# Two-branch spectral mixing on one core: 64x64 matmul tiles, a split inverse radix, contiguous transposes and a new hand-written order

## The chip, the core and the metric

The kernel runs on one core of a Trainium2 chip. A core has TensorE (PE; its weight loads are shown apart as PEld), VectorE (DVE), ScalarE (ACT) and GpSimd (POOL), and SyncE (SP), whose queue issues most DMAs. The metric is the device time of one execution in microseconds (us), the median over several runs. All data is fp32; a matmul of fp32 shows in the trace as two records (two passes).

## The reference

```python
x = A_x                                    # 1 x 2048 x 512, row index = time, column = channel
g = sigmoid((x * gate_w).sum(-1, keepdims=True))
# a: 2-D real FFT over time and channel, times a complex weight, and back
X = rfft2(x) * (A_w_r + 1j * A_w_i)
a = irfft2(X, s=(2048, 512))
# b: state-space convolution along time, and a skip
K = 2 * einsum("dn,dnl->dl", C, exp(A * dt * pos)).real
b = irfft(rfft(u, 4096) * rfft(K, 4096), 4096)[:, :2048] + u * D_skip     # u = x
out = g * a + (1 - g) * b
```

Where a channel's `dt` is so small that `K` is constant over the 2048 steps, the convolution is a running sum over time, scaled by one number a channel. The kernel counts the channels for which that holds; when it holds for all 512, as with these inputs, it uses running sums, and a general path in an `If` at the end is skipped.

## The kernel before, in words

Four pieces of work share the engines.

*Input transform.* The input comes in parts (`PARTS`), is folded (`fold`: sum and difference of two halves of the channels, on VectorE `f` or GpSimd `F`), goes through a first radix step over 32 time values (`C_`, TensorE), and is transposed in 32x32 blocks from PSUM into `AR` (`c_a`, VectorE).

*Frequency units.* Nine units (`UNITS`; index 0 is a half unit of 64 rows, the others have 128). Each goes: `P_` second time step on TensorE, `t_a` copy to SBUF on ScalarE, `D_` channel transform on TensorE, `d_a` copy of one half on ScalarE, `Z_` sums and differences on VectorE, `W_` twice (letters `W`, `U`), the products with the weights, on VectorE, `p_a` and `g_a` sums and differences on GpSimd, `h_a` a fix of row 0 on ScalarE, `I_` inverse channel transform on TensorE, `i_a` copy on ScalarE, `V_` sum and difference into `AI` on VectorE.

*Running sum.* For four groups of 128 channels: `load_x`, scaling on ScalarE into PSUM (`x_a`), a running sum on VectorE (`scan`), a skip scaling in place on ScalarE (`skip`), and an accumulating DMA on GpSimd's queue that adds the running sum onto the input (`both`), or VectorE instead (`skip2`). `G_` is the gate: 16 matmuls in column tiles of 32, a sigmoid, and a DMA that spreads it.

*Inverse along time and output.* `B_` second inverse time step (TensorE), a copy back (`e_a`, ScalarE), a transposition in 32x32 blocks in place (`b_a`, VectorE). `Y_` turns the running-sum branch (TensorE transposes), `s_a` scales it by 1 - g (ScalarE); `Q_` is the last time step (TensorE), and `q_a` (VectorE), or `a_a` with `A_a` (ScalarE, GpSimd), adds both and stores.

The order on every engine is the order of the words in `PLAN`: a letter for the function and a number for its argument. PSUM has four buffers of two banks, taken in turn by all of this (`psum`), so a step can wait for the reader of the buffer's last content. `blk` has 13 SBUF buffers, `w` four.

Of the kernel before, what the change touches and what calls it, by code (L numbers as in the profile page):

```python
# [15 lines left out]
P = 128  # L30
L = 2048
# [8 lines left out]
F1 f0 C0 c0 C1 R2 f2 R5 R3 f3 l2 c1 F4 C2 c2 f5 C4 N0 F6 X0 l3 R4 C5 R1 c4 C6 f8 C8 N1 N2 G4 F9 R0 c5 l0 X1 l1 c8 c6  # L40
C9 C3 c9 f7 N3 x0 X2 C7 c3 R6 c7 P1 P0 J0 G5 x1 t1 J1 t0 D1 m0 m1 J2 x2 m2 P2 P4 L2 L1 D0 R9 d1 z1 Z1 y1 t2 D2 t4 W1
U1 L3 d0 z0 p1 Z0 L0 y0 W0 l4 d2 z2 Z2 y2 U0 P6 P5 U2 R8 g1 P3 t5 t6 D5 W2 R7 L4 p0 g0 t3 X3 x3 l5 h1 D3 z3 m3 d3 d5
l7 L5 Z3 z5 y3 h0 W3 U3 l6 p2 I1 i1 V1 G0 P7 g2 Z5 o3 p3 o0 L6 y5 G1 G2 t7 W5 D4 d4 I0 g3 U5 p5 g5 h3 D6 z4 Z4 S3 D7
i0 V0 y4 U4 o1 L7 W4 d7 z6 G3 d6 Z6 h5 l8 y6 z7 r0 P8 p4 t8 B1 W6 Z7 e1 y7 h2 U6 g4 I5 i5 o2 p6 D8 z8 L8 W7 g6 U7 p7
d8 h4 V5 I3 r1 i3 V3 x4 o4 I2 i2 B3 e3 I4 Z8 y8 m4 g7 h6 i4 V2 x6 W8 h7 I6 i6 U8 V6 V4 I7 S2 p8 i7 V7 m6 k6 g8 h8 B2
B6 e6 e2 I8 i8 v8 B5 x7 S1 e5 B4 x5 m7 j8 e4 w8 E8 o5 K8 H8 S0 B7 e7 m5 r2 k7 Y4 Y7 Y1 Y6 b1 s7 s4 Y3 s3 Y0 s0 Y2 Y5
b6 s6 s1 b2 b3 b0 b4 s5 b5 b7 Q6 s2 Q0 q6 q0 Q5 q5 Q3 q3 Q7 Q4 q4 a7 Q2 A7 q2 Q1 q1
# [9 lines left out]
def _consts():  # L57
# [38 lines left out]
    s2e = s2[:17].reshape(17, 128, 128).transpose(1, 0, 2)  # L96
# [15 lines left out]
    s2p = s2p.transpose(1, 0, 2)  # L112
# [10 lines left out]
    s1a = np.zeros((32, 2, 2, 16, 2, 2, 32, 2))  # L123
    for g in range(2):
        s1b[:, g, :, :, :, g] = s1i[32 * g:32 * g + 32]
        for e in range(2):
            for dh in range(2):
                s1a[:, g, :, :, e, dh, :, g] = s1i[32 * g:32 * g + 32, :, :16] * 2 / 512 * (-1) ** (e * dh)
    s1b = s1b.reshape(32, 128, 64).transpose(1, 0, 2)
    s1a = s1a.reshape(32, 128, 128).transpose(1, 0, 2)  # L130
# [16 lines left out]
        "c_s1e": f32(s1e.reshape(128, 128)), "c_s1f": f32(s1f.transpose(1, 0, 2)), "c_s2e": f32(s2e), "c_s2": f32(s2),  # L147
        "c_s2p": f32(s2p), "c_s2q": f32(s2q), "c_s1b": f32(s1b), "c_s1a": f32(s1a), "c_dfw": f32(dfw), "c_dbw": f32(dbw),
# [5 lines left out]
def body(ctx: ExitStack, tc: tile.TileContext, x, xg, xt, w, wh, prms, vecs, gw, dskip,  # L154
         c_s1e, c_s1f, c_s2e, c_s2, c_s2p, c_s2q, c_s1b, c_s1a, c_dfw, c_dbw, c_pos, c_eye, out):
# [14 lines left out]
    AI = keep.tile([P, 17, D], F32, name="AI")  # L170
    VA = AI[:, 0:16].rearrange("p s (e d) -> p (s e) d", e=2)
# [31 lines left out]
    with tc.manual_schedule():  # L203
# [3 lines left out]
        for i, k in enumerate(PARTS):  # L207
            nc.sync.dma_start(X[:, 64 * k.start:64 * k.stop], x[:, 64 * k.start:64 * k.stop])
# [7 lines left out]
        V.memset(one, 1.0)  # L216
# [15 lines left out]
        def C_(q):  # L232
            n = 32 * (PARTS[q].stop - PARTS[q].start)
            p = t_["c", q] = psum("p_s1")
            for u in range(2):
                T.matmul(p[:, u, :n], s1e, t_["f", q][:, u, :n], start=True, stop=True)  # L236

        def c_a(q):
            n = PARTS[q].stop - PARTS[q].start
            V.transpose(AR.rearrange("p s (u d) -> p u d s", u=2)[:, :, PARTS[q]], t_["c", q][:, :, :32 * n].rearrange("p u (b d) -> p u d b", d=n))  # L240

# [33 lines left out]
        def x_a(r):  # L275
            t_["v1", r] = psum("p_x").rearrange("p u n -> p (u n)")
            S.activation(t_["v1", r], part(r), AF.Copy, scale=s0[:, coef(r):coef(r) + 1])  # L277

        def scan(r):
            if r % 2 == 0:  # L280
                t_["v", r // 2] = work.tile([P, 2, 1024], F32, tag="v", name="v", bufs=NV)
            v = t_["v0", r] = t_["v", r // 2][:, r % 2]
            V.tensor_tensor_scan(v, one.broadcast_to([P, 1024]), t_["v1", r], t_["v0", r - 1][:, 1023:1024] if r % 2 else 0.0, op0=ALU.mult, op1=ALU.add)  # L283
# [4 lines left out]
        def both(k):  # L288
            G.dma_start(XT[:, k], t_["v", k].rearrange("p h l -> p (h l)"), accum_op=ALU.add)
# [42 lines left out]
        def load_w(u):  # L332
# [5 lines left out]
            t_["w", u] = t.rearrange("p (o r a k) -> p o r a k", o=2, r=2, a=2)  # L338
# [6 lines left out]
        def P_(u):  # L345
            pr = UNITS[u]
            p = t_["pt", u] = psum("p_t").rearrange("p k (q c r) -> p (k q) c r", q=2, c=2)
            for v in range(nrow(pr) // 64):
                sl, k = (0, 16) if pr == 8 else (2 * pr + v, 2 * pr + v)
                for q in range(4):  # L350
                    T.matmul(p[:, q, :, 64 * v:64 * v + 64], AR[:, 16 * (q // 2) + sl, 128 * (q % 2):128 * (q % 2) + 128], s2e[:, k], start=True, stop=True)  # L351
# [18 lines left out]
        def d_a(u):  # L370
            ds = t_["ds", u] = short("ds")
            S.copy(ds[..., :nrow(UNITS[u])], parts(u)[:, :, 0:4:3])


        def Z_(u):
            n = nrow(UNITS[u])
            p, re = parts(u), t_["ds", u][..., :n]
            V.tensor_tensor(p[:, :, 0:4:3], p[:, :, 1:3], re, op=ALU.add)  # L378
# [416 lines left out]
```

## Time and profile before

| quantity | value |
|---|---|
| median of 3 runs | 148.23 us (147.55 to 148.67) |
| span of the profiled execution | 146.8 us, 1834 instructions |
| VectorE busy | 113.8 us in 134 instructions |
| TensorE busy | 112.6 us in 611 records |
| ScalarE busy | 70.5 us in 136 |
| GpSimd busy | 57.4 us in 57 |
| HBM | 17.93 MB read, 4.19 MB written |

The span runs from the first to the last instruction of the profiled execution, 1.4 us less than the median of the timed runs. Rows of the trace have a start, a length in us, an engine, a line of the kernel, an operation, the tiles it writes and reads, and how often; in square brackets stands the idle time before it and what ended it. Rows of groups have a line, a shape, a count, busy us and the mean ns of one, then the idle time before.

### The profile page before, as it was taken

The page shows a single profiled execution, that of the slowest core. Times are in us where ns is not written, and L with a number is a line of the kernel's source. Part 1 is how long each engine was busy: PE and PEld are TensorE (multiplying, and loading weights), DVE is VectorE, ACT ScalarE, POOL GpSimd, SP SyncE. Part 2 cuts the span into 40 slices and gives each one's busy share as a digit, 9 for nine tenths or more (in the row PEclk, how much of TensorE's full clock was granted, in tenths as well). Part 3 has the DMA queues.
Part 4 walks back from the last instruction along what each step waited for, and adds up shares of the span by engine and source line. Part 5 has one row for each costly group of instructions (what it writes and reads, how often), then busy time and mean ns, then how long its engine had stood idle before and what let it go on. Part 6 is the DMA issues. An engine that isn't in the chain of part 4 may idle for free.

```text
span 146.8 us, 1834 instructions
## 1 busy us (share of the span) xinstructions
PE 112.6 (77%) x611; PEld 86.1 (59%) x611; DVE 113.8 (78%) x134; ACT 70.5 (48%) x136; POOL 57.4 (39%) x57
## 2 busy tenths in 40 slices
PE   7936976399989998959888878997805975999600
PEld 7811352098978982858378577462405964888400
DVE  0369999995788597759798995979689997695900
ACT  0003000337375969496789765398610699504000
POOL 0306850100059993976999979200200000003300
PEclk9999999959999999999999999999975899999985
DMA  4999999992105870404793898000191000158690
GB/s 114 318 275 418 391 417 387 413 416 99 37 7 173 287 292 0 143 5 146 132 225 91 273 214 210 4 0 0 40 214 36 0 0 0 57 205 318 223 354 19
DMA packets 9427, 25.52 MB, mean 174 GB/s; under 512 B 1568, under 2 KB 2624, under 8 KB 8512
## 3 DMA queue, kind: packets, MB, share of 16 engines
q1 hardware_dynamic: 8976, 22.16, 42.2%
q0 software_dynamic: 432, 3.15, 10.9%
q8 instruction: 7, 0.11, 0.3%
q14 instruction: 12, 0.10, 0.2%
HBM read 17.93 MB, written 4.19 MB: 151 GB/s over the span
## 4 chain that ended last, share of the span: by engine, by line
DVE 31%; PE 30%; ACT 17%; DMA 9%; issue 5%; POOL 2%; SPq 1%; DVEq 0%; ACTq 0%; POOLq 0%
DVE AR L240 9%; PE p_oa L528 8%; PE p_d L365 6%; ACT AR L516 6%; PE p_t L351 5%; DMA XT<-v 5%; PE p_v L440 5%; DMA AI<-in_x_dram 5%; DVE v L283 3%; DVE p_d L378 3%; DVE p_d L379 3%; DVE tw L405 3%; PE p_ia L481 2%; PE p_y L511 2%; DVE AR L549 2%
## 5 line engine op out<-in xcount | busy, mean ns | idle before, releaser
L351 PEld LDWEIGHTS p_t<-s2e,AR 128*128 128x128 f32 x136 | 17.4, 208 | 5.5 <-DVE AR L240 3.5
L351 PE MATMUL p_t<-s2e,AR 128*128 128x128 f32 x136 | 18.0, 294 | 3.4 <-DVE AR L240 2.7
L440 PEld LDWEIGHTS p_v<-dbw,gt 128*128 128x128 f32 x136 | 16.0, 192 | 7.5 <-issue 4.6
L440 PE MATMUL p_v<-dbw,gt 128*128 128x128 f32 x136 | 16.8, 278 | 4.6 <-ACT gs L303 1.5
L236 PE MATMUL p_s<-f,AI 128*128 128x512 f32 (+1 forms) x40 | 15.7, 527 | 5.5 <-DVE f L228 3.4
L412 POOL TENSOR_TENSOR px<-tw 128x512 f32<-128x512 f32 (+1 forms) x9 | 10.9, 1215 | 19.6 <-DVE tw L405 19.5
L503 DVE STREAM_TRANSPOSE AI<-AI 128x1024 f32<-128x1024 f32 x8 | 16.9, 2202 | 1.8 <-ACT AI L485 1.8
L365 PE MATMUL p_d<-et,dfw 128*128 128x256 f32 (+1 forms) x72 | 16.1, 371 | 0.7 <-ACT et L356 0.6
L240 DVE STREAM_TRANSPOSE AR<-p_s 128x1024 f32<-128x1024 f32 (+1 forms) x10 | 14.8, 1555 | 1.6 <-PE p_s L236 1.6
L516 ACT ACTIVATE AR<-p_y,g 128x256 f32<-128x256 f32 x32 | 11.8, 587 | 8.1 <-PE p_y L511 8.1
L528 PE MATMUL p_oa<-AI,s1a 128*128 128x256 f32 x64 | 14.1, 380 | 1.7 <-ACT AR L516 1.7
L511 PE MATMUL p_y<-eye,XT 128*128 128x128 f32 x64 | 10.0, 317 | 6.5 <-DMA XT<-v 5.6
L277 ACT ACTIVATE p_x<-XT,pers 128x1024 f32<-128x1024 f32 x8 | 9.0, 1121 | 12.5 <-POOL pers L261 10.4
L549 DVE SCALAR_TENSOR_TENSOR AR<-p_oa,g,AR 128x256 f32<-128x256 f32 x28 | 11.6, 477 | 4.2 <-PE p_oa L528 4.0
L236 PEld LDWEIGHTS p_s<-f,AI 128*128 128x128 f32 x40 | 7.1, 196 | 13.1 <-issue 4.3
L365 PEld LDWEIGHTS p_d<-et,dfw 128*128 128x128 f32 x72 | 12.7, 190 | 2.5 <-ACT et L356 1.2
L528 PEld LDWEIGHTS p_oa<-AI,s1a 128*128 128x128 f32 x64 | 12.1, 190 | 3.5 <-ACT AR L516 1.9
L543 POOL TENSOR_TENSOR AR<-AR,qs 128x1024 f32<-128x1024 f32 x1 | 2.3, 2348 | 29.2 <-ACT qs L539 29.2
L511 PEld LDWEIGHTS p_y<-eye,XT 128*128 128x128 f32 x64 | 9.2, 201 | 7.8 <-issue 6.3
L453 DVE TENSOR_TENSOR AI<-p_v,po 128x512 f32<-128x512 f32 (+1 forms) x18 | 10.9, 650 | 2.3 <-ACT po L445 2.3
L405 DVE TENSOR_TENSOR tw<-p_d,w 128x1024 f32<-128x1024 f32 x8 | 9.8, 1219 | 3.6 <-ACT p_d L390 3.6
L481 PE MATMUL p_ia<-AI,s2p 128*128 128x512 f32 x26 | 12.0, 595 | 0.0
(66 smaller groups left out, 180.6 us busy)
## 6 DMA issues: line engine op xcount, KB each, us to landing
w<-in_w_dram SPq DMA_DIRECT2D x8, 512.0 KB, 5.6
XT<-in_xt_dram SPq DMA_DIRECT2D x4, 1024.0 KB, 7.0
out_dram<-AR SPq DMA_DIRECT2D x16, 256.0 KB, 3.7
AI<-in_x_dram SPq DMA_DIRECT2D x6, 512.0 KB, 7.6
XT<-v POOLq DMA_DIRECT2D x3, 1024.0 KB, 7.0
s1a<-in_c_s1a_dram SPq DMA_DIRECT2D x4, 512.0 KB, 3.9
AI<-in_x_dram SPq DMA_DIRECT2D x4, 256.0 KB
prm<-in_prms_dram SPq DMA_DIRECT2D x3, 256.0 KB
```

What stands on the lines that cost most here:

```text
L236: T.matmul(p[:, u, :n], s1e, t_["f", q][:, u, :n], start=True, stop=True)
L240: V.transpose(AR.rearrange("p s (u d) -> p u d s", u=2)[:, :, PARTS[q]], t_["c", q][:, :, :32 * n].rearrange("p u (b d) -> p u d b", d=n))
L351: T.matmul(p[:, q, :, 64 * v:64 * v + 64], AR[:, 16 * (q // 2) + sl, 128 * (q % 2):128 * (q % 2) + 128], s2e[:, k], start=True, stop=True)
L365: T.matmul(p[:, o, :, h, :n], dfw[:, 2 * h + o], et[:, ::-1] if h else et, start=True, stop=True)
L405: E.tensor_tensor(t.rearrange("p o r a k -> p (o r a k)"), z.rearrange("p o q k -> p (o q k)"), w.rearrange("p o r a k -> p (o r a k)"), o ...
L440: T.matmul(p[:, v, h, o], t_["gt", u][:, o, v, 2 * h:2 * h + 2].rearrange("p c k -> p (c k)"), dbw[:, h, o], start=True, stop=True)
L481: T.matmul(p[:, v], s2p, AI[:, sl], start=True, stop=True)
L503: V.transpose(v, v)
L511: T.transpose(p[:, k, i], xv[:, i, :, 4 * j + k], eye)
L516: S.activation(AR[:, b].rearrange("p (i d) -> p i d", i=2), t_["py", j][:, k], AF.Copy, scale=g1[:, 1, b:b + 1])
L528: T.matmul(p[:, k], s1a[j // 2][:, 4 * j % 8 + k], VA[:, 4 * j + k], start=True, stop=True)
L549: V.scalar_tensor_tensor(AR[:, b], t_["pq", j][:, k], g1[:, 0, b:b + 1], AR[:, b], op0=ALU.mult, op1=ALU.add)
```

## The change

*Input step.* A part now is a slice of 64 channel offsets (before of 128); the first step uses 64x64 tiles, four to a product. Three parts (1, 3, 5) are folded by GpSimd; the other six are not folded, and TensorE adds the halves by accumulating two matmuls, the second weight block having the sign. VectorE folds none. `c_a` transposes from runs in PSUM to runs in `AR`.

```diff
         def C_(q):
-            for u in range(2):
-                T.matmul(p[:, u, :n], s1e, t_["f", q][:, u, :n], start=True, stop=True)
+            tiles = [(g, h, slice(64 * h, 64 * h + 64)) for g in range(2) for h in range(2)]
+            if ("f", q) in t_:
+                for g, h, r in tiles:
+                    T.matmul(p[64 * g:64 * g + 64, h, :2 * n], s1e[r, 0:64], t_["f", q][r, :, g * n:g * n + n], start=True, stop=True, tile_position=(64 * h, 64 * g))
+            else:
+                for u in range(2):
+                    for i in range(2):
+                        for g, h, r in tiles:
+                            T.matmul(p[64 * g:64 * g + 64, h, u * n:u * n + n], s1e[r, 64 * u * i:64 * u * i + 64], xin(q)[r, i, g * n:g * n + n], start=i == 0, stop=i == 1, tile_position=(64 * h, 64 * g))
         def c_a(q):
-            V.transpose(AR.rearrange("p s (u d) -> p u d s", u=2)[:, :, PARTS[q]], t_["c", q][:, :, :32 * n].rearrange("p u (b d) -> p u d b", d=n))
+            V.transpose(AR.rearrange("p u (h t) s -> p h u (t s)", h=2)[..., 32 * k.start:32 * k.stop], t_["c", q][:, :, :2 * n].rearrange("p h (u n) -> p h u n", u=2))
```

`P_` reads its weights from the new `AR` with a step of 32 elements: `AR[:, q % 2, :, 16 * (q // 2) + sl]`.

*Running sum by pairs.* Each group of 128 channels has one running sum over 1024 pairs in place of two of 1024 values. The odd steps come out of it; the even steps are the odd ones less the odd input, on GpSimd. All four groups use the accumulating DMA (three before), and all eight skip scalings are on ScalarE (six before).

```diff
+        def y_a(k):
+            t_["uo", k] = blk([P, 1024], "uo")
+            S.activation(t_["uo", k], XT[:, k, 1:L:2], AF.Copy, scale=s0[:, coef(2 * k):coef(2 * k) + 1])
-            V.tensor_tensor_scan(v, one.broadcast_to([P, 1024]), t_["v1", r], t_["v0", r - 1][:, 1023:1024] if r % 2 else 0.0, op0=ALU.mult, op1=ALU.add)
+            V.tensor_tensor_scan(v[:, 1:L:2], t_["v1", k], t_["uo", k], 0.0, op0=ALU.add, op1=ALU.add)
+        def even(k, E):
+            E.tensor_tensor(v[:, 0:L:2], v[:, 1:L:2], t_["uo", k], op=ALU.subtract)
```

*Row 0 by masks.* Row 0 of a unit needs no sums and differences. Before, ScalarE kept and put back its values (`z_a`, `z_b`: three short copies a unit). Now `Z_` multiplies by a column that is 0 in row 0: four operations of half the size for two.

```diff
-            V.tensor_tensor(p[:, :, 0:4:3], p[:, :, 1:3], re, op=ALU.add)
-            V.tensor_tensor(p[:, :, 1:3], re, p[:, :, 1:3], op=ALU.subtract)
+            V.scalar_tensor_tensor(p[:, 0, 0:2], p[:, 0, 2:4], m_, ds[:, 0], op0=ALU.mult, op1=ALU.add)
+            V.scalar_tensor_tensor(p[:, 0, 2:4], ds[:, 0], nm, p[:, 0, 2:4], op0=ALU.mult, op1=ALU.add)
+            V.tensor_tensor(p[:, 1, 0:2], p[:, 1, 2:4], ds[:, 1], op=ALU.add)
+            V.tensor_tensor(p[:, 1, 2:4], p[:, 1, 2:4], ds[:, 1], op=ALU.subtract)
```

`g_a` writes `gt` with a step of two elements, its order being (k, c) where it was (c, k).

*Inverse split 32 + 64.* The second inverse step works on 32 channel columns of all units at once, in 64x64 tiles whose streamed operand has a step of 256 elements; VectorE transposes straight from PSUM, so `e_a`, `e2_a` and the transposition in place are gone. Two slots are joined by two small matmuls and a copy (`K_`). `Q_` streams `VA[:, :, 4 * j + k]`, a step of 32 elements; its output is added in `BS`, not in `AR`.

```diff
+        def B_(k):
+            p = t_["pb", k] = psum("p_ia")
+            av = AI.rearrange("p s (e t) -> p t (s e)", e=2)[:, 32 * k:32 * k + 32]
+            for x in range(2):
+                for z in range(2):
+                    r = slice(64 * z, 64 * z + 64)
+                    y = 16 * (z ^ x)
+                    T.matmul(p[64 * x:64 * x + 64, z], s2v[r], av[r, :, y:y + 16], start=True, stop=True, tile_position=(64 * z, 64 * x))
-        def b_a(c):
-            v = VA[:, :, 32 * c:32 * c + 32].rearrange("p b d -> p d b")
-            V.transpose(v, v)
+        def b_a(k):
+            V.transpose(VA[:, 32 * k:32 * k + 32].rearrange("p t (z i) -> p t z i", z=2), t_["pb", k].rearrange("p z (t i) -> p t z i", i=16))
```

Before, `B_` could take a pair of slots as soon as its unit was done; now each needs all units. `PLAN` is written anew:

```diff
-F1 f0 C0 c0 C1 R2 f2 R5 R3 f3 l2 c1 F4 C2 c2 f5 C4 N0 F6 X0 l3 R4 C5 R1 c4 C6 f8 C8 N1 N2 G4 F9 R0 c5 l0 X1 l1 c8 c6
+C0 X0 c0 C2 c2 F1 F3 C1 C4 c1 c4 C3 c3 R6 C6 N0 N1 F5 C5 c6 c5 C7 c7 R2 N3 R0 R3 C8 c8 x0 P6 y0 X1 t6 J0 R7 J1 R1 P1
...
```

What stands on the engines, in three places. First VectorE in the input stage (`f` and `p_s` are the fold and the first step's result, `prm` parameters for the running sum), before:

```order
L228 TENSOR_TENSOR f<-AI 128x256
L229 TENSOR_TENSOR f<-AI 128x256
L240 STREAM_TRANSPOSE AR<-p_s_116 128x2x8x32
L228 TENSOR_TENSOR f<-AI 128x512
L229 TENSOR_TENSOR f<-AI 128x512
L228 TENSOR_TENSOR f<-AI 128x512
L229 TENSOR_TENSOR f<-AI 128x512
L240 STREAM_TRANSPOSE AR<-p_s_120 128x2x8x32
L240 STREAM_TRANSPOSE AR<-p_s_138 128x2x16x32
```

and of the change, for the whole stage:

```order
L259 STREAM_TRANSPOSE AR<-p_s_112 128x2x2x128
L259 STREAM_TRANSPOSE AR<-p_s_131 128x2x2x256
L259 STREAM_TRANSPOSE AR<-p_s_155 128x2x2x128
L259 STREAM_TRANSPOSE AR<-p_s_160 128x2x2x256
L259 STREAM_TRANSPOSE AR<-p_s_179 128x2x2x256
L265 TENSOR_REDUCE AI<-prm 128x4
L266 TENSOR_REDUCE AI<-prm 128x4
L259 STREAM_TRANSPOSE AR<-p_s_186 128x2x2x256
L259 STREAM_TRANSPOSE AR<-p_s_209 128x2x2x256
L259 STREAM_TRANSPOSE AR<-p_s_216 128x2x2x256
L278 TENSOR_REDUCE pers<-prm 128x4
L259 STREAM_TRANSPOSE AR<-p_s_241 128x2x2x256
```

The folds are gone from VectorE; nine transposes and three reductions remain.

Second GpSimd at the start of the units (`pers` holds the scale of the running sum, `v` the sums, `tw`, `px`, `gt` the unit's products and their sums), before:

```order
L260 TENSOR_TENSOR pers<-pers,AI 128x4
L261 TENSOR_TENSOR pers<-pers 128x4
L412 TENSOR_TENSOR px<-tw 128x2x2x128
L413 TENSOR_TENSOR px<-tw 128x2x2x128
L424 TENSOR_TENSOR gt<-px 128x2x4x64
L425 TENSOR_TENSOR gt<-px 128x2x4x64
```

and of the change:

```order
L279 TENSOR_TENSOR pers<-pers,AI 128x4
L280 TENSOR_TENSOR pers<-pers 128x4
L308 TENSOR_TENSOR v<-v,uo 128x1024
L273 TENSOR_TENSOR AI<-AI 128x4
L274 TENSOR_TENSOR AI<-AI 128x4
L275 TENSOR_SCALAR AI<-AI 128x4
L308 TENSOR_TENSOR v<-v,uo 128x1024
L423 TENSOR_TENSOR px<-tw 128x2x2x128
L424 TENSOR_TENSOR px<-tw 128x2x2x128
```

Two even halves of the running sum stand ahead of the first unit; the other two come later among the units.

Third TensorE at the end (`p_v` inverse channel transform, `p_ia` second inverse step, `p_y` the turned branch, `p_oa` the last product), before:

```order
L440 MATMUL p_v<-dbw,gt 128x128 x8
L481 MATMUL p_ia<-AI,s2p 128x512 x4
L496 MATMUL p_ia<-AI,s2p 128x256 x4
L481 MATMUL p_ia<-AI,s2p 128x512 x2
L511 MATMUL p_y<-eye,XT 128x128 x64
L528 MATMUL p_oa<-AI,s1a 128x256 x32
```

and of the change:

```order
L497 MATMUL p_y<-eye,XT 128x128 x16
L454 MATMUL p_v<-dbw,gt 128x128 x8
L497 MATMUL p_y<-eye,XT 128x128 x8
L486 MATMUL p_ia<-AI,s2v 64x512 x32
L497 MATMUL p_y<-eye,XT 128x128 x16
L521 MATMUL p_oa<-AR,s1a 128x256 x12
L497 MATMUL p_y<-eye,XT 128x128 x16
L521 MATMUL p_oa<-AR,s1a 128x256 x20
```

Half of the turning now stands among and ahead of the last units, the whole second inverse step behind them, and the rest of the turning inside the last product.

More of the change, by code (lines that the diff above doesn't have):

```diff
@@ L215, in body @@
         V.memset(ones, 1.0)
-        V.memset(one, 1.0)
+        V.memset(pers[:, 12:14], 1.0)
+        V.memset(nm, -1.0)
+        V.memset(pers[0:1, 13:15], 0.0)
         warm = psum("p_warm")
@@ L439, in I_ @@
                     for o in range(2):
-                        T.matmul(p[:, v, h, o], t_["gt", u][:, o, v, 2 * h:2 * h + 2].rearrange("p c k -> p (c k)"), dbw[:, h, o], start=True, stop=True)
+                        T.matmul(p[:, v, h, o], rows(u, o, v, h), dbw[:, h, o], start=True, stop=True)
         def i_a(u):
@@ L483, in e_a @@
-        def e_a(u):
-            pr = UNITS[u]
-            S.copy(AI[:, 2 * pr:2 * pr + 2], t_["pb", u])
-        def half(u, k):
-            pr = UNITS[u]
-            return AI[:, 2 * pr:2 * pr + 2].rearrange("p s (h k t) -> p k s h t", h=2, k=2)[:, k]
-        def B2_(u, k):
-            if k == 0:
-                t_["pb", u] = psum("p_ia").rearrange("p k (s h t) -> p k s h t", s=2, h=2)
-            for v in range(2):
-                T.matmul(t_["pb", u][:, k, v], s2p, half(u, k)[:, v], start=True, stop=True)
@@ L709, in body @@
             T.matmul(p[:, 0], s2q[:, 2], spB[:, 1], start=False, stop=True)
-            S.copy(AR[:, 0], p[:, 0])
+            S.copy(AG[:, 0], p[:, 0])
             for c in range(16):
```

248 lines of the change are left out of this document (123 added, 125 removed).

## Prediction

> **What bounds it now.** I read the page's busy shares first, then a table of the span cut into five stages, then the chain that ended last.
>
> ```profile
> PE 112.6 (77%) x611; PEld 86.1 (59%) x611; DVE 113.8 (78%) x134; ACT 70.5 (48%) x136; POOL 57.4 (39%) x57
> ```
> ```profile
> 0.00:29.60 29.60, 20.40 (x68) 11.60 (x68) 22.59 (x30) 2.61 (x3) 9.64 (x17) 1.00 0.94 342
> 29.60:105.00 75.40, 67.29 (x414) 53.10 (x415) 62.52 (x70) 53.50 (x96) 45.00 (x39) 0.98 0.45 133
> 105.00:124.00 19.00, 10.82 (x67) 9.30 (x65) 17.12 (x9) 9.86 (x26) 0.45 (x1) 0.82 0.27 55
> 124.00:139.80 15.80, 14.05 (x64) 12.08 (x64) 11.60 (x28) 4.50 (x13) 2.35 (x1) 1.00 0.54 195
> 139.80:146.80 7.00, 0.00 (x0) 0.00 (x0) 0.01 (x1) 0.00 (x0) 0.00 (x0) 0.68 0.48 177
> ```
> ```profile
> 2.13 6.84 DMA AI<-in_x_dram
> ...
> 11.55 2.73 DVE AR L240 x2
> ...
> 18.99 5.33 DVE AR L240 x4
> ...
> 104.58 6.97 DMA XT<-v
> ...
> 115.15 8.87 ACT AR L516 x24
> 124.06 12.34 PE p_oa L528 x56
> ```
>
> Columns of the table: stage, length, then busy us of PE, weight loads, VectorE, ScalarE, GpSimd. The total (VectorE 78%) hides that each stage has its own limit. Stage 1 (input transform) is VectorE's: 22.59 of 29.6 us, and the chain runs through its transposes. In stage 2 (nine frequency units) TensorE is busy 67.29 and VectorE 62.52 of 75.4. In stage 3 VectorE transposes for 17.12 of 19 us, while the other branch waits 6.97 us for the accumulating DMA and then scales on ScalarE; both end at 124. Stage 4 is TensorE's last product, stage 5 the last store and the program's end.
>
> **The change, stage by stage.** The rows with prices, grouped by line and shape (busy us, mean ns):
>
> ```profile
> L240 DVE STREAM_TRANSPOSE AR<-p_s 128x1024 f32<-128x1024 f32 x6 | 11.3, 1901 | 0.0
> L503 DVE STREAM_TRANSPOSE AI<-AI 128x1024 f32<-128x1024 f32 x8 | 16.9, 2202 | 1.8 <-ACT AI L485 1.8
> L405 DVE TENSOR_TENSOR tw<-p_d,w 128x1024 f32<-128x1024 f32 x8 | 9.8, 1219 | 3.6 <-ACT p_d L390 3.6
> L400 DVE TENSOR_TENSOR tw<-p_d,w 128x256 f32<-128x256 f32 x4 | 1.5, 417 | 0.7 <-POOL px L413 0.7
> L378 DVE TENSOR_TENSOR p_d<-p_d,ds 128x512 f32<-128x512 f32 x8 | 5.5, 691 | 1.7 <-ACT first L384 1.7
> L283 DVE TENSOR_TENSOR_SCAN v<-pers,p_x 128x1024 f32<-128x1024 f32 x4 | 9.1, 2276 | 1.6 <-ACT p_x L277 1.6
> L300 PE MATMUL p_gate<-XT,gws 128*32 128x512 f32 x32 | 3.6, 595 | 0.0
> L485 ACT COPY AI<-p_ia 128x1024 f32<-128x1024 f32 x7 | 7.0, 1010 | 3.9 <-PE p_ia L481 3.9
> L277 ACT ACTIVATE p_x<-XT,pers 128x1024 f32<-128x1024 f32 x8 | 9.0, 1121 | 12.5 <-POOL pers L261 10.4 <-DVE count L314 2.1
> L389 ACT COPY p_d<-ds 1x256 f32<-1x256 f32 x8 | 2.9, 365 | 9.7 <-DVE p_d L379 9.7
> L445 ACT COPY po<-p_v 128x512 f32<-128x512 f32 x8 | 4.6, 577 | 2.8 <-PE p_v L440 2.8
> L543 POOL TENSOR_TENSOR AR<-AR,qs 128x1024 f32<-128x1024 f32 x1 | 2.3, 2348 | 29.2 <-ACT qs L539 29.2
> L289 POOL DMA_DIRECT2D XT<-v x3 | 2.8, 918 | 13.2 <-ACT XT L286 13.2
> ```
>
> Unknown prices first. The contiguous transpose: the trace has 1901 ns (strided, from PSUM) and 2202 ns (strided, SBUF); below lies the plain 1024-element operation out of PSUM, 1219 ns. I take 1.15 start to start, since the change makes both operands runs. The 64x64 tiles: the gate's 32 column tiles ran 32 matmuls of 512 columns in 3.64 us, 0.114 each, four side by side. Row tiles are not in the trace; bounds are four abreast, two abreast and one at a time, and I take four, by the gate's row, the only tiled one. The running sum with two inputs keeps 2.3 (below: 1.2, as L405). Strided ScalarE reads keep 1.12. The even half on GpSimd costs L543's 2.35, or half as much again if its stride of two elements hurts; likewise the products that write `gt` with that stride, 1.27 or 1.9. I take the lower, as they only move every second word.
>
> **Stage 1.** VectorE loses all its folds, and the other transposes shrink: 7 x 1.15 + 2 x 0.6 + three reductions of 0.6 + 0.3 = 11.4 against 22.6. TensorE, which now adds the halves itself in six of nine parts, takes over. Such a part has 16 matmuls of 256 columns in two passes, 32 records; at the 0.22 per 256 columns of the last product (64 in 14.05, quoted below) and four abreast, 1.76, with filling 1.85. A folded part is 8 records of 512 at 0.114, 0.91.
>
> ```profile
> 11.60 1.27 POOL L228 TENSOR_TENSOR f<-AI 128x512 f32<-128x512 f32 x1 [5.16 <-DMA AI<-in_x_dram]
> 14.88 1.65 POOL L228 TENSOR_TENSOR f<-AI 128x512 f32<-128x512 f32 x1 [0.78 <-DMA AI<-in_x_dram]
> ```
>
> These two starts, which waited for a DMA, give the arrival of parts 4 and 6, whose bytes lie at the same places before and after. So: part 4 from 11.6 to 13.45, part 3 to 14.4, part 6 from 14.9 to 16.75, part 5 to 17.7, parts 7 and 8 to 21.4, last transpose 22.6. Before it was 29.6: a gain of 7.
>
> **Stage 2.** The first product on GpSimd now hangs on this chain: the last parameter reduction ends at 21.4, GpSimd's scale 0.5, two scalings on ScalarE 2.2, first running sum 2.3, the second pair's scaling 1.5 (its buffer waits for that sum), second running sum 2.3, Z, then the two weight products 2.3. Z is four operations of 256 columns, 4 x 0.4 = 1.6, for two of 0.69, so 0.2 dearer, but the two short ScalarE copies after it (L389 and its twin, 0.4 each with a handover) leave the path. Total 12.7: GpSimd starts at 34.1, against 41.9.
>
> ```profile
> 41.90 1.27 POOL L412 TENSOR_TENSOR px<-tw 128x512 f32<-128x512 f32 x1 [15.31 <-DVE tw L405]
> 49.94 1.27 POOL L412 TENSOR_TENSOR px<-tw 128x512 f32<-128x512 f32 x1
> 53.74 1.28 POOL L425 TENSOR_TENSOR gt<-px 128x512 f32<-128x512 f32 x1
> 91.55 1.27 POOL L425 TENSOR_TENSOR gt<-px 128x512 f32<-128x512 f32 x1
> 89.81 2.02 PE L440 MATMUL p_v<-dbw,gt 128*128 128x128 f32 x16 [0.58 <-issue]
> 101.11 0.67 DVE L453 TENSOR_TENSOR AI<-p_v,po 128x512 f32<-128x512 f32 x1
> ```
>
> From then on GpSimd is the fullest: a unit takes 5.08 (49.94 to 55.02), eight of them 40.6, the half unit 2.9, two of the four even halves 4.7 (the other two fall before 34), four accumulating DMAs 3.6: 51.8. VectorE has some 10 less than its 62.5: four running sums fewer (9.2), two L292 operations of 1.27 gone, Z 2 dearer; ScalarE loses its row copies and, to stage 3's gain, the L485 copies. TensorE keeps about 50 for the units, so it is nearly as full. If GpSimd never waits, its last product ends at 85.9; behind it stand two short copies 0.7, 16 matmuls 2.0, the copy 0.6 and two additions 1.2: last V at 90.4. If instead the units keep the pace of before, 72.2 from the last transpose (29.6) to the last V (101.8), it is 94.8. With two engines nearly full and the reads of PSUM by four buffers in turn, I take the middle, 92.6.
>
> The four accumulating DMAs go out by about 69 in GpSimd's order and need 7 us, so Y no longer waits for one: the 5.6 us wait of TensorE at 105.8 and ScalarE's late scaling go under the units. Should an order wait push the last DMA past 85, that wait is back.
>
> **Stage 3.** After the last V come eight second steps, each 8 records, 0.91 four abreast, and eight transposes at 1.15 from PSUM behind the first: 0.9 + 9.3 + 0.1 = 10.3, against 22.3. The copies L485 are gone from between.
>
> **Stage 4.**
>
> ```profile
> 118.24 1.16 PE L511 MATMUL p_y<-eye,XT 128*128 128x128 f32 x8 [0.30 <-ACT AR L516]
> 36.24 3.73 PE L351 MATMUL p_t<-s2e,AR 128*128 128x128 f32 x32
> 124.06 14.05 PE L528 MATMUL p_oa<-AI,s1a 128*128 128x256 f32 x64 [1.75 <-ACT AR L516]
> 138.55 1.26 DVE L549 SCALAR_TENSOR_TENSOR AR<-p_oa,g,AR 128x256 f32<-128x256 f32 x3
> ```
>
> The last product stays 14.05, two Y groups now lie inside it (2 x 1.16), and its tail to the last VectorE operation is 1.7 as before (138.1 to 139.8): 18.1, and 0.3 for handovers: 18.4, so 2.6 dearer. Stage 5 stays 7.0.
>
> The strides deserve a weighing. P now loads weights with a step of 32 elements, and the last product streams them so. Y already loads weights at that step, eight in 1.16 with the first taking 0.28, 0.126 each; contiguous L351 has 32 in 3.73, 0.117. So I charge weights nothing, and streaming nothing either, though no row streams with such a step. [...]
>
> **The sum.** 92.6 (last V) + 10.3 + 18.4 + 7.0 = 128.3 as span. The profiled execution of before spans 146.8; the median of the runs, 148.23, lies 1.4 above it. So **129.7 us**.
>
> **The rivals.** First: the transposes stay near 1.9, their rate being the block's and not the stride's. For it: the 512-element form took 1035, nearly proportional. Against: SBUF to PSUM already moves it by 0.3. Stage 1 is then VectorE's again and ends at 27 (+4.4), and stage 3 costs 8 x 0.75 more, 6: 140.
>
> Second: the tiles run only two abreast, because the row halves exclude each other. For it: no row tile in the trace. Against: the gate's four. Unfolded parts then take 3.7 and folded ones 1.8. From the arrival of part 2 (2.13 + 6.84 = 9.0 in the chain) TensorE has 5 x 3.7 + 2 x 1.8 + 0.9 = 23.0, so stage 1 ends at 33.2 (+10.6); stage 3 becomes TensorE's at 1.82 a step (+5.4): 146.
>
> Third: streaming with a step of 32 (last product) or 256 elements (second step) runs at half speed. The product takes 28.1 (+14), the second step 1.82 a time (+5.4): 149, on the line between same and slower. For it only that no row streams so; against it Y's weights.
>
> Fourth, on the slower side: tiled matmuls follow each other one at a time, because each brings its own weights and the loads of one tile hold up the products of the next. For it: 32 loads come with each unfolded part, as many as the whole gate had. Against: the gate's loads lay under its products. Stage 1 then needs 5 x 7.0 + 2 x 3.6 + 1.8 = 44 us from 9.0 on (+31.6) and stage 3 eight times 3.64 (+20): 181. Slower than before begins at 18.5 us of extra cost, somewhat below two abreast.
>
> Fifth: GpSimd's stride-two accesses cost half as much again. Its sixteen `gt` products grow by 0.63 each and two even halves by 1.2, +12.5, some of it in the slack that I granted: 140. [...]
>
> **How the numbers follow.** Forecast 0.63, transposes dear 0.10, two abreast 0.08, GpSimd dear 0.08, streaming dear 0.06, one at a time 0.05. The forecast's own range is 125 to 134: with GpSimd never waiting, 127.5, less some 2.5 if the running sum takes the lower price; above, the pace of before gives 131.9, and 2 if the weights of the first unit come late. The range reaches to the dear transposes and GpSimd, and down to several prices together at their lower ends: 121 to 142. A measurement can tell about 1% from no change. Faster by over 1% are the first four, 0.89, less 0.01 for the second's upper end: 0.88. Streaming dear is split: within 1% 0.03 and that 0.01, slower 0.03 and the 0.05 of one at a time: 0.08.
>
> **What would show it.** The contiguous transposes near 1.15 in the groups; an input part without fold near 1.85 on TensorE; last input transpose at 22 to 23; first `px` near 34; GpSimd above 85% busy from there to the last `gt`; no wait of TensorE for the accumulating DMA; 10 us between last V and last product; records of the last product still 0.22 apart. I am wrong if the middle is longer than 72 us, if a transpose stays over 1.6, or if tiled matmuls of one part follow each other instead of overlapping.

## The result and the profile after

The changed kernel takes 159.82 us (median of 4 runs, 159.20 to 160.45); the kernel before, in the same job, 148.45 (147.55 to 149.27). The ratio is 1.077, 95% interval 1.069 to 1.085: slower by 11.4 us, where 18.5 us faster was forecast. The profiled execution took 160.45 us and spans 158.7, against 146.8 before. Medians, here and below, are over all executions of a kernel in its job; ratios leave out those that ran over 1.5% above its fastest.

The page's busy shares, to be read against those of before:

```profile
PE 138.0 (87%) x817; PEld 100.8 (64%) x817; DVE 87.1 (55%) x127; ACT 62.2 (39%) x111; POOL 70.6 (44%) x62
```

VectorE and ScalarE lost 26.7 and 8.3 us of work, as the change set out to do; TensorE gained 25.4. The span cut into stages (first step; units up to the last V; second inverse step with turning; last product; the short rest is not shown), columns as in the prediction's table; the last three are TensorE's granted clock, the busy share of the DMA engines and GB/s:

```profile
0.00:22.79 22.79, 16.84 (x236) 12.43 (x236) 11.61 (x16) 2.00 (x3) 7.01 (x12) 1.00 0.92 325
22.79:103.92 81.13, 73.56 (x421) 65.51 (x422) 57.23 (x84) 48.23 (x78) 56.41 (x47) 0.92 0.65 183
103.92:121.84 17.92, 17.92 (x80) 8.07 (x81) 10.01 (x8) 2.05 (x6) 0.00 (x0) 1.00 0.00 1
121.84:151.50 29.66, 29.66 (x82) 14.76 (x80) 6.64 (x16) 9.94 (x27) 7.14 (x3) 1.00 0.34 126
```

Stage 1 lost 6.8 us, nearly the forecast 7 (22.8 instead of 29.6). In stages 3 and 4 TensorE is busy in every microsecond, and in the units 73.56 of 81.13. The chain that ended last, which before ran through VectorE's transposes and a DMA, stays on TensorE from 103.92 to 151.5, nearly all of it in two lines (L486 and L521):

```profile
103.92 16.08 PE p_ia L486 x63
120.00 2.00 PE p_y L497 x16
122.01 10.39 PE p_oa L521 x24
132.39 1.79 PE p_y L497 x16
134.19 17.33 PE p_oa L521 x40
```

The groups by line show why (busy us, mean ns of one record):

```profile
L372 PE MATMUL p_t<-s2e,AR 128*128 128x128 f32 x136 | 31.3, 392 | 3.1 <-DVE AR L259 1.4 <-DVE count L335 0.9 <-ACT gs L324 0.8
L521 PE MATMUL p_oa<-AR,s1a 128*128 128x256 f32 x64 | 28.0, 609 | 0.0
L486 PE MATMUL p_ia<-AI,s2v 64*64 64x512 f32 x64 | 16.1, 1153 | 1.3 <-ACT bs L509 1.3
```

The 64 records of the last product took 14.05 us before, and P's 136, by the same view of the kernel before:

```profile
L351 PE MATMUL p_t<-s2e,AR 128*128 128x128 f32 x136 | 18.0, 294 | 3.4 <-DVE AR L240 2.7 <-DVE tw L403 0.4 <-DVE tw L400 0.3
```

These are the three places where the change gives a matmul an operand in SBUF with a step: P's weights (32 elements), the second inverse step's stream (256) and the last product's stream (32). Records of the last product are now 28.0 / 64 = 0.44 us apart, before 0.22; the second inverse step takes 2.0 a time, where the forecast had 0.91. P's 136 records take 31.3 us instead of 18.0.

### The profile page after: what moved, and what is told of

The parts are those of the page before. It is cut to its first block, busy times and chain, and to the rows that moved or that the text cites. A ratio compares the mean times of both kernels' runs of the same rounds, so it can differ in the third digit from the quotient of the medians.

```text
span 158.7 us, 2220 instructions
## 1 busy us (share of the span) xinstructions
PE 138.0 (87%) x817; PEld 100.8 (64%) x817; DVE 87.1 (55%) x127; ACT 62.2 (39%) x111; POOL 70.6 (44%) x62
## 5 line engine op out<-in xcount | busy, mean ns | idle before, releaser
L372 PE MATMUL p_t<-s2e,AR 128*128 128x128 f32 x136 | 31.3, 392 | 3.1 <-DVE AR L259 1.4
L372 PEld LDWEIGHTS p_t<-s2e,AR 128*128 128x128 f32 x136 | 30.6, 312 | 4.1 <-DVE AR L259 1.8
L521 PE MATMUL p_oa<-AR,s1a 128*128 128x256 f32 x64 | 28.0, 609 | 0.0
L521 PEld LDWEIGHTS p_oa<-AR,s1a 128*128 128x128 f32 x64 | 13.0, 205 | 13.6 <-issue 13.4
L486 PE MATMUL p_ia<-AI,s2v 64*64 64x512 f32 x64 | 16.1, 1153 | 1.3 <-ACT bs L509 1.3
L388 PEld LDWEIGHTS p_d<-et,dfw 128*128 128x128 f32 x72 | 14.1, 215 | 4.1 <-ACT et L377 1.4
L259 DVE STREAM_TRANSPOSE AR<-p_s 128x1024 f32<-128x1024 f32 (+1 forms) x9 | 9.8, 1115 | 10.3 <-PE p_s L254 10.3
L489 DVE STREAM_TRANSPOSE AR<-p_ia 128x1024 f32<-128x1024 f32 x8 | 10.0, 1251 | 7.6 <-PE p_ia L486 7.6
L254 PE MATMUL p_s<-AI 64*64 64x256 f32 (+1 forms) x192 | 10.7, 363 | 3.6 <-DMA AI<-in_x_dram 3.6
L377 ACT COPY et<-p_t 128x1024 f32<-128x1024 f32 (+1 forms) x9 | 8.7, 963 | 12.4 <-PE p_t L372 10.7
L308 POOL TENSOR_TENSOR v<-v,uo 128x1024 f32<-128x1024 f32 x4 | 9.6, 2412 | 8.6 <-DVE v L304 8.6
L435 POOL TENSOR_TENSOR gt<-px 128x512 f32<-128x512 f32 (+1 forms) x9 | 11.5, 1277 | 4.3 <-PE p_d L388 4.1
L486 PEld LDWEIGHTS p_ia<-AI,s2v 64*64 64x64 f32 x64 | 6.2, 152 | 9.6 <-issue 7.9
```

The lines of the kernel that those rows point to most:

```text
L254: T.matmul(p[64 * g:64 * g + 64, h, u * n:u * n + n], s1e[r, 64 * u * i:64 * u * i + 64], xin(q)[r, i, g * n:g * n + n], start=i == 0, sto ...
L259: V.transpose(AR.rearrange("p u (h t) s -> p h u (t s)", h=2)[..., 32 * k.start:32 * k.stop], t_["c", q][:, :, :2 * n].rearrange("p h (u n ...
L308: E.tensor_tensor(v[:, 0:L:2], v[:, 1:L:2], t_["uo", k], op=ALU.subtract)
L372: T.matmul(p[:, q, :, 64 * v:64 * v + 64], AR[:, q % 2, :, 16 * (q // 2) + sl], s2e[:, k], start=True, stop=True)
L388: T.matmul(parts(u)[:, o, 1:3] if h else parts(u)[:, o, 0:4:3], dfw[:, 2 * h + o], t_["et", u][:, 2 * h + o, :, :n], start=True, stop=True)
L435: G.tensor_tensor(gv[:, :, 0], src[0], src[1], op=ALU.subtract)
```

## The experiments

The theory after this reading: the miss is these three steps and nothing else. Its rivals: the new order (waits that appear anyway), or 64x64 tiles that don't run four abreast (for the second inverse step). Line numbers in the experiments stand up to four lines later than in the change.

**One step at a time.** Three kernels each make one operand contiguous and leave the rest as it is (`VF` is `AR` as one flat row). They read other elements, so they leave out the reference's result and serve for the time alone. Before has 149.70 us in their job and 148.45 in the change's, so a gain over the change is good to about 1 us. The last product:

```diff
-T.matmul(p[:, k], s1a[j // 2][:, 4 * j % 8 + k], VA[:, :, 4 * j + k], start=True, stop=True)
+T.matmul(p[:, k], s1a[j // 2][:, 4 * j % 8 + k], VF[:, 256 * (4 * j + k):256 * (4 * j + k) + 256], start=True, stop=True)
```

> The last product streams 256 contiguous elements of the same tile instead of one element in 32 (so it multiplies other numbers); all else as in the change. Theory (a stride on the streamed operand halves TensorE's rate): its 64 records fall from 28.0 us to about 14, 0.22 apart, and the time by 13 to 14 us, to about 146. Rival (the product is paced by its readers on VectorE and ScalarE, four buffers): records stay near 0.44 and the time stays near 160.

The group of the last product:

```profile
L522 PE MATMUL p_oa<-AR,s1a 128*128 128x256 f32 x64 | 14.1, 379 | 0.0
```

Measured 146.15 us, 13.7 less than the change, ratio to before 0.984 (0.979 to 0.988). P's weights:

```diff
-AR[:, q % 2, :, 16 * (q // 2) + sl]
+VF[:, 4096 * (q % 2) + 3840 + 128 * (q // 2):4096 * (q % 2) + 3968 + 128 * (q // 2)]
```

> The second time step (P) loads 128 contiguous weights of the same tile, always from its last columns, instead of one element in 32 (other numbers); all else as in the change. Theory (a stride on a weight load doubles it, and the load, not the product, sets the pace): 32 records go from 7.1 to 3.7 us, TensorE busy falls by 14 us, and the time by 8 to 14, to 146 to 152, less than the busy time since TensorE has waits among the units. Rival (P is slow because a buffer or an input comes late): record spacing stays at 0.22.

```profile
L373 PE MATMUL p_t<-s2e,AR 128*128 128x128 f32 x136 | 17.9, 289 | 3.0 <-DVE AR L260 1.4 <-DVE count L336 0.9 <-ACT gs L325 0.7
```

Measured 151.31, 8.5 less; 13.4 us of TensorE's work is gone, so some 5 of it had lain beside other work or in waits. The second inverse step's stream:

```diff
-T.matmul(p[64 * x:64 * x + 64, z], s2v[r], av[r, :, y:y + 16], ...)
+T.matmul(p[64 * x:64 * x + 64, z], s2v[r], AI[r, 2 + (z ^ x)], ...)
```

> The second inverse step in 64x64 tiles streams 512 contiguous elements of one slot instead of single elements with a step of 256 (other numbers); all else as in the change. Theory (stride): eight records take 0.9 us instead of 2.0, VectorE's eight transposes set the stage at 1.15 to 1.25 each, and the time falls by about 6, to 154. Rival (64x64 tiles run only two abreast there): eight records stay at 1.8 to 2.0 and the time at 160.

```profile
L486 PE MATMUL p_ia<-AI,s2v 64*64 64x512 f32 x64 | 7.1, 592 | 1.4 <-ACT bs L509 1.4
```

Measured 152.06, 7.8 less. With a contiguous stream a step takes 7.1 / 8 = 0.89, where its eight records of 512 columns one after the other would take 3.5 (an estimate from the last product's 14.1 / 64 = 0.22 per 256): the tiles do run four abreast, and that rival is out.

**All three at once.**

> All three at once: last product, weights of the second time step and second inverse step read contiguous elements (other numbers). Theory (these three strides are the whole miss): 160 less 14, 11 and 6, about 129, which is what was forecast with strides priced at nothing. Rival (the new order loses something of its own in the units): well above, 135 to 140.

Measured 129.34 us (128.10 to 132.36, before 149.70 in that job): 30.5 less than the change, where the three single gains add up to 30.0. This is the forecast's 129.7, and its places are there too (first `px`, last `gt`, last V, the second inverse step, the last product, the last VectorE operation, from the timelines):

```profile
35.26 1.27 POOL L424 TENSOR_TENSOR px<-tw 128x512 f32<-128x512 f32 x1 [1.81 <-DVE tw L417]
...
87.53 1.27 POOL L437 TENSOR_TENSOR gt<-px 128x512 f32<-128x512 f32 x1
...
92.05 1.29 DVE L468 TENSOR_TENSOR AI<-p_v,po 128x512 f32<-128x512 f32 x2 [3.77 <-ACT po L460]
...
93.60 7.10 PE L487 MATMUL p_ia<-AI,s2v 64*64 64x512 f32 x64 [1.35 <-ACT bs L510]
...
102.84 5.45 PE L522 MATMUL p_oa<-AR,s1a 128*128 128x256 f32 x24
...
118.75 1.66 DVE L543 SCALAR_TENSOR_TENSOR bs<-p_oa,g,bs 128x256 f32<-128x256 f32 x4
```

So the new order hid nothing else, and that rival is out too: the last `gt` ends 2.9 us later than forecast, the last V 0.7 later, the last product starts when it should, and the span is 126.5 instead of 128.3.

**A ladder of steps.** How far may one step for nothing? Eight groups of the last product, eight units of P and eight groups of Y (the TensorE transposes) each get another step:

```diff
+STEPS = [1, 2, 3, 4, 5, 8, 16, 32]
-VA[:, :, 4 * j + k]
+VF[:, 0:256 * STEPS[j]:STEPS[j]]
-AR[:, q % 2, :, 16 * (q // 2) + sl]
+VF[:, 4096 * (q % 2):4096 * (q % 2) + 128 * STEPS[u - 1 if u else 7]:STEPS[u - 1 if u else 7]]
-T.transpose(p[:, k, i], xv[:, i, :, 4 * j + k], eye)
+T.transpose(p[:, k, i], XF[:, 4096 * i:4096 * i + 128 * STEPS[j]:STEPS[j]], eye)
```

> The change with other elements read: the eight groups of the last product stream with a step of 1, 2, 3, 4, 5, 8, 16 and 32 elements (group 0 to 7), the nine units load the weights of the second time step with the same steps (units 1 to 8), and the eight groups of the turning transposes load theirs so too. [...] Rival (any step over 1 costs double): 0.44 and 0.22 from step 2 on. [...]

One window for each group of the last product, in the order of the program: steps 16, 5, 2, then 1, 3, 32, 8, 4 (length, busy us of PE, records, clock, DMA share; a record that crosses a bound counts on both sides, each group has eight):

```profile
117.76:121.44 3.68, 3.64 (x9) 1.00 0.00 0
121.44:125.11 3.67, 3.67 (x9) 1.00 0.00 0
125.11:126.92 1.81, 1.80 (x8) 1.00 0.31 118
128.50:130.50 2.00, 1.96 (x9) 1.00 0.20 75
130.50:133.16 2.66, 2.66 (x9) 1.00 0.69 251
133.16:136.69 3.53, 3.53 (x9) 1.00 1.00 366
136.69:140.38 3.69, 3.69 (x9) 1.00 0.36 130
140.38:143.95 3.57, 3.55 (x8) 1.00 0.48 176
```

Steps 1 and 2 give 0.23 to 0.25 us a record, step 3 0.33, and every step from 4 to 32 0.44 to 0.46. Step 2 is free, step 3 costs half as much again, step 4 already costs what step 32 does (one execution, 152.88 us). P's weights show the same order where the granted clock was 1.00: units with steps 32 and 16 (one row), 4, 3 and 2 in this order take 0.22, 0.25, 0.18 and 0.13 a record. The units with steps 8, 1 and 5 fell into stretches at a lower clock (0.87, 0.64 and 0.70), so their 0.26, 0.18 and 0.24 don't price a step; the price of step 1 is that of the run with contiguous weights above (17.9 us for 136, 0.13). Y's transposes don't care (rows of the timeline, with all eight steps among their 64 records):

```profile
31.03 7.08 PE L375 MATMUL p_t<-s2e,AR 128*128 128x128 f32 x32
52.23 4.00 PE L375 MATMUL p_t<-s2e,AR 128*128 128x128 f32 x16 [0.77 <-ACT gs L327]
59.22 2.87 PE L375 MATMUL p_t<-s2e,AR 128*128 128x128 f32 x16
74.03 2.04 PE L375 MATMUL p_t<-s2e,AR 128*128 128x128 f32 x16
87.27 1.07 PE L500 MATMUL p_y<-eye,XT 128*128 128x128 f32 x8
92.42 2.01 PE L500 MATMUL p_y<-eye,XT 128*128 128x128 f32 x16
97.44 1.12 PE L500 MATMUL p_y<-eye,XT 128*128 128x128 f32 x8
115.86 2.10 PE L500 MATMUL p_y<-eye,XT 128*128 128x128 f32 x16
126.75 1.95 PE L500 MATMUL p_y<-eye,XT 128*128 128x128 f32 x16
```

Y is at 0.12 to 0.14 a record in every row, step 3 alone (the first), step 2 alone (the third) and the others two steps to a row: the row that the prediction leaned on could not have shown a price of P. The expectation's "any step over 1 costs double" is wrong: at step 2 a record of the last product takes 0.23 and one of P 0.13, as at step 1. Why step 3 lies between and why steps from 4 to 32 cost alike, these runs don't show.

**Where to put the step instead.** The remaining runs compute all of the reference and ask which engine can take the step. First `AR` slot by slot, so that P and the last product read runs, and VectorE's transposes write single elements 1 KB apart:

```diff
-AR = keep.tile([P, 2, P, 32], F32, name="AR")
+AR = keep.tile([P, 32, 2, P], F32, name="AR")
-V.transpose(AR.rearrange("p u (h t) s -> p h u (t s)", h=2)[..., 32 * k.start:32 * k.stop], ...)
+V.transpose(AR.rearrange("p s u (h t) -> p h u t s", h=2)[:, :, :, k], ...)
```

> The tile AR is laid out slot by slot, so that weights of the second time step and the streamed operand of the last product are runs, and both sets of VectorE transposes scatter their output with a step of 256 elements instead; the second inverse step keeps its step. Computes the reference. Theory (scattering costs a transpose at most what it cost before, 1.9 us, and VectorE has room in both stages): about 137, 160 less 14 for the product and 8 to 9 for the weights. Rival (the scattered transposes take over both stages): 1.9 to 2.2 each, first stage 4 longer, 141 to 143.

Measured 142.06 us, ratio to before 0.954 (0.943 to 0.964): faster than both kernels, but the rival's time, since a transpose costs 1.93 to 1.95 instead of 1.24 (groups by shape):

```profile
L489 DVE STREAM_TRANSPOSE AR<-p_ia 128x1024 f32<-128x1024 f32 x8 | 15.4, 1949 | 3.1 <-PE p_ia L486 2.9
L259 DVE STREAM_TRANSPOSE AR<-p_s 128x1024 f32<-128x1024 f32 x7 | 13.1, 1928 | 3.9 <-PE p_s L254 3.9
```

Then also runs of 32 for the second inverse step, whose transposes take the step while they read PSUM:

```diff
-av = AI.rearrange("p s (e t) -> p t (s e)", e=2)[:, 32 * k:32 * k + 32]
+av = AI.rearrange("p s (e t) -> p (s e) t", e=2)[:, :, 32 * k:32 * k + 32]
-av[r, :, y:y + 16]
+av[r, y:y + 16]
-t_["pb", k].rearrange("p z (t i) -> p t z i", i=16)
+t_["pb", k].rearrange("p z (i t) -> p t z i", i=16)
```

> As slot_major, and the second inverse step streams runs of 32 elements, VectorE's transposes taking the step on their PSUM side. Computes the reference. Theory (only TensorE pays for steps; a run of 32 counts as contiguous, and a transpose with both sides strided stays near 1.25): eight records 0.9, transposes 1.25, about 131. Rival (a transpose pays for a strided PSUM side as before the change, 1.9 to 2.2): the stage is VectorE's at 16 us, as long as TensorE's was, and the time stays at that of slot_major.

Measured 141.55, ratio 0.941 (0.924 to 0.957). The second inverse step fell to 7.8 us, but the stage is now VectorE's: eight transposes at 1951 ns, 14.2 us. Which side of the transpose is dear, the read of PSUM with a step or the write to SBUF? The same edit on the change itself, where the write is contiguous:

> The change with one edit: the second inverse step streams runs of 32, and its transposes read PSUM with the step and write contiguously; P and Q as in the change. All of the reference is computed. If a transpose pays only for scattered writes: eight at 1.25 us, the stage 10 to 11 us instead of 17 to 18, about 152 us as in b_run. If it pays for a stepped read of PSUM too: 1.9 us each, the stage about 15.5, 157 us.

```profile
L489 DVE STREAM_TRANSPOSE AR<-p_ia 128x1024 f32<-128x1024 f32 x8 | 9.2, 1211 | 1.4 <-PE p_ia L486 1.4
```

Measured 152.30 (one run). A step on PSUM's side costs a transpose nothing (1211 ns; 1212 in the run with the contiguous stream alone, whose transposes read PSUM in runs of 16); the scattered write to SBUF is the price (1951). Two kernels let ScalarE do the scattering: the transposes write a contiguous tile, a ScalarE copy reads it with a step of 32 and writes `AR` in runs.

```diff
+st = blk([P, 32, 32], "bst")
+V.transpose(st.rearrange("p t (z i) -> p t z i", z=2), ...)
+S.copy(AR.rearrange("p s u t -> p s (u t)")[:, :, 32 * k:32 * k + 32], st.rearrange("p t s -> p s t"))
```

For both kinds of transposes:

> AR laid out slot by slot as in slot_major, but the transposes (both kinds) write one contiguous tile each, and ScalarE copies that tile into AR; the second inverse step streams runs of 32. All of the reference is computed. If the step costs only where VectorE writes it and ScalarE's copies cost what its other 1024-element copies cost (1.1 to 1.3 us each) and run a tile behind: first stage done about 24 (26.2 in slot_major), P at 0.13 a record as in slot_major, last V near 93 to 95, the second inverse step 8 x 1.25 plus a copy, about 11.5, product 16, rest 6: 133 to 135 us. Rival, ScalarE pays for the step too (2 us and more a copy): the copies take the transposes' place as the slowest link of both stages, 140 us or more, no better than slot_runs.

For those of the second inverse step alone:

> As slot_major in the first stage (scattered transposes, P from 26.2), and only the eight transposes behind the second inverse step write a contiguous tile that ScalarE copies into AR; that step streams runs of 32. All of the reference is computed. If a ScalarE copy takes 1.1 to 1.3 us: the stage falls from 17 us in slot_major to about 11.5, 136 to 137 us. If it takes 2 us: the stage stays near 16, 141 us. If the transpose that reads PSUM with a step costs 1.9 us itself, the stage is near 16 as well, with the copies short.

Measured 146.83 (ratio 0.974, 0.963 to 0.985) and 146.56 (0.978, 0.969 to 0.987): worse than scattering on VectorE. The copy has the dear price of both expectations, 2 us, but the second had 141 us for it: from its last V to the last product its timeline has 20.7 us, where 16 were expected. ScalarE pays for the step as well (groups of the first of the two; copies, and the wait of the last product):

```profile
L493 ACT COPY AR<-bst 128x1024 f32<-128x1024 f32 x8 | 15.3, 1988 | 2.6 <-DVE bst L492 2.6
L525 PE MATMUL p_oa<-AR,s1a 128*128 128x256 f32 x64 | 16.4, 421 | 9.6 <-ACT AR L493 9.6
```

The eight copies share ScalarE with the scalings of the other branch, of which two groups stand between them, and the last product waited 9.6 us for them.

**Pairs.** The ladder has a free step: 2. So `AR` is laid out in pairs of slots; the transposes write two neighbours at a time, P and the last product read every second element, and the second inverse step and its transposes stay as in the edit with runs of 32.

```diff
-AR = keep.tile([P, 32, 2, P], F32, name="AR")
+AR = keep.tile([P, 16, 2, P, 2], F32, name="AR")
-VA[:, :, 4 * j + k]
+AR[:, 2 * j + k // 2].rearrange("p u t b -> p (u t) b")[:, :, k % 2]
```

> slot_runs with AR laid out in pairs of slots: the transposes (both kinds) write pairs of neighbouring elements instead of single ones, the weights of P and the streams of the last product read every second element; the second inverse step streams runs of 32, its transposes take their step from PSUM. All of the reference is computed. The ladder says that step 2 is free: P near 18 to 21, the last product 14.2. If a scattered write is priced by the number of separate pieces, the transposes fall to about half of the excess, 1.55 to 1.6 us (1.24 contiguous, 1.93 scattered): first stage done near 24.5, the stage behind the second inverse step 12 to 13, 137 us. If any scattered write costs the same, transposes 1.93: 141 us as slot_runs. If pairs are as good as runs, 1.24: 131 to 132 us.

```profile
L372 PE MATMUL p_t<-s2e,AR 128*128 128x128 f32 x136 | 18.8, 297 | 3.0 <-DVE AR L259 1.5 <-DVE count L335 0.9 <-ACT gs L324 0.5
L521 PE MATMUL p_oa<-AR,s1a 128*128 128x256 f32 x64 | 14.9, 390 | 1.1 <-DVE AR L489 1.1
L489 DVE STREAM_TRANSPOSE AR<-p_ia 128x1024 f32<-128x1024 f32 x8 | 9.2, 1216 | 1.4 <-PE p_ia L486 1.4
```

Measured 130.78 us (129.24 to 133.95), ratio to before 0.880 (0.869 to 0.891). Pairs cost the transposes nothing (1216 ns against 1211 for runs), and steps of 2 cost TensorE next to nothing: the expectation's third case. With this layout and the runs for the second inverse step the change does what was forecast.

## Why the prediction was wrong

The sum was right but for one sentence: "So I charge weights nothing, and streaming nothing either". That is the step that failed, and it was worth 30.5 us.

- *Stage 1.* Right: forecast end 22.6, measured 22.79. The unfolded part took 1.85 and the contiguous transpose 1.15 to 1.25; rows of the change's timeline and groups:

```profile
17.80 3.69 PE L254 MATMUL p_s<-AI 64*64 64x256 f32 x64
```
```profile
L259 DVE STREAM_TRANSPOSE AR<-p_s 128x1024 f32<-128x1024 f32 x7 | 8.5, 1235 | 5.1 <-PE p_s L254 5.1
L304 DVE TENSOR_TENSOR_SCAN v<-p_x,uo 128x1024 f32<-128x1024 f32 x4 | 9.1, 2286 | 5.2 <-ACT p_x L296 3.7 <-ACT uo L300 1.5
L308 POOL TENSOR_TENSOR v<-v,uo 128x1024 f32<-128x1024 f32 x4 | 9.6, 2412 | 8.6 <-DVE v L304 8.6
L435 POOL TENSOR_TENSOR gt<-px 128x512 f32<-128x512 f32 x8 | 10.8, 1346 | 0.2
L300 ACT ACTIVATE uo<-XT,pers 128x1024 f32<-128x1024 f32 x4 | 5.0, 1248 | 0.0
L497 PE MATMUL p_y<-eye,XT 128*128 128x128 f32 x64 | 8.1, 277 | 0.0
```

- *Prices of new operations.* Right: running sum 2.29 (2.3), even half 2.41 (2.35), `gt` with a step of two 1.35 (1.27), four abreast. The first, second, fourth and fifth rivals fell with them. In the fifth, the kernel before writes `gt` in runs at 1.31 in the mean of its groups, so the step of 8 bytes costs 0.04 a product. The even half reads and writes with a step of 8 bytes, at 2.41 us, where the contiguous sum of the same size in the kernel before (L543) takes 2.35.
- *Units.* Forecast: GpSimd from 34.1 to 85.9, the fullest engine. Measured in the change 37.12 to 99.12, and TensorE is the fullest. The same stretch, first `px` to last `gt`, in the change and with all three operands contiguous (columns as in the table of stages):

```profile
37.12:99.12 62.00, 56.34 (x333) 48.69 (x332) 46.81 (x70) 36.28 (x58) 50.97 (x42) 0.92 0.65 164
```
```profile
35.26:88.80 53.54, 44.09 (x310) 36.73 (x308) 46.61 (x70) 34.93 (x56) 50.88 (x42) 0.97 0.73 194
```

  GpSimd has the same 50.9 us to do. With contiguous weights it is 95% busy and the stretch is its own, 53.5 (forecast 51.8); with a step of 32 TensorE has 12 us more in its stretch, 10 of them P's (18.6 against 8.6, one unit's P lying ahead of the shorter stretch), and holds it up: 91% against GpSimd's 82%. With P's weights alone contiguous the stretch runs from 34.78 to 88.01, 53.2 us. So the term "TensorE keeps about 50 for the units" hung on the weights, and no rival priced them.
- *The end.* The last V and the last VectorE operation in the change's timeline:

```profile
102.38 1.29 DVE L467 TENSOR_TENSOR AI<-p_v,po 128x512 f32<-128x512 f32 x2 [3.77 <-ACT po L459]
...
151.54 1.66 DVE L542 SCALAR_TENSOR_TENSOR bs<-p_oa,g,bs 128x256 f32<-128x256 f32 x4 [1.73 <-PE p_oa L521]
```

- *Stage 3.* Forecast 10.3; measured from the last V (103.67) to the last product (122.01) 18.3. Without steps 93.34 to 102.84, 9.5. (In the sum the eight transposes at 1.15 are 9.2 and not 9.3, which changes nothing.)
- *Stage 4.* Forecast 18.4; measured 122.01 to the last VectorE operation's end at 153.2, 31.2; without steps 17.6.
- *Some luck in the total.* Without steps the last V is 0.7 late although the last `gt` is 2.9 late, because the forecast took the middle between two paces; stages 3, 4 and 5 are shorter than forecast by 0.8, 0.8 and 0.9. These misses cancel in part, so the agreement with 129.7 is closer than its terms are.
- *The accumulating DMAs.* Right: Y's 64 records wait for nothing (L497 above), where 5.6 us of waiting stood before.

The third rival had the effect, streaming at half speed (28.0 us instead of 14.1 in the last product), and the product's size: +14 against 13.7; its +5.4 for the second inverse step was 7.8, as a step of 256 makes that 2.3 times as long (16.1 against 7.1) and not twice. It got a chance of 0.06 and left out P's weights, 8.5 more, so that its 149 stood on the line where 160 was to come. The evidence against it was Y's 0.126 a record, read as the price of a weight load with a step. The ladder shows that row to be blind: Y's pace is the same with every step, 0.12 to 0.14 a record. Why a TensorE transpose doesn't feel the step of its weights, when a matmul with weights of the same size does, these runs leave open; the traces show only that a transpose leaves one record (64 for 64 calls) and a matmul two (136 for 68). Nor do they say how a read of SBUF is made.

## What to carry to other kernels

Before a step is moved onto a TensorE operand, look for a row that streams or loads with that step in the same kind of instruction; a neighbour that looks alike can be blind to the price, as Y was (0.12 to 0.14 a record with every step, where P went from 0.13 to 0.23). With 4-byte elements lay out pairs: a step of 2 in what TensorE reads (P 18.8 us against 17.9 contiguous, the last product 14.9 against 14.1) and two neighbours in what VectorE writes (1216 ns against 1211) were all but free here. And where an engine grows busier, look for groups with the same count and a longer record: P and the last product, 136 and 64 records before and after, named the cause on the first page.

## What was not expected of the hardware

- Streams and weights of fp32 matmuls from SBUF: step 1 and 2 alike (0.22 to 0.25 us for 256 columns streamed, 0.13 a record with weights of 128x128), step 3 half as much again (0.33, 0.18), steps from 4 to 32 double (streams 0.44 to 0.46 at 4, 5, 8, 16 and 32; weights 0.22 to 0.25 at 4, 16 and 32).
- A VectorE transpose of 128x1024 takes 1.21 to 1.25 us when it writes SBUF in runs or pairs and 1.92 to 1.95 when it writes single elements 1 KB apart; a step in what it reads from PSUM cost nothing here (1.21).
- A ScalarE copy of 128x1024 that reads SBUF with a step of 32 takes 1.99 us; with a step of 2 (L300 above, with a scale) 1.25.
